# Joining the float32 work of TensorE into longer groups, with a new order of the front

## The chip, the cores and the metric

The kernel runs on one core of a Trainium2 chip. The core has a matrix engine (PE, with its weight loads shown apart as PEld), a vector engine (DVE), a scalar engine (ACT), GpSimd (POOL) and SyncE (SP), whose queue here issues most of the transfers. The metric is device time in microseconds (us) of one execution, as the median over several executions.

## The reference

Three stages follow one another on 8 x 576 = 4608 tokens. First comes a two-step attention with 8 heads of width 64, then a product of two projections, then a two-layer network:

```
p_packed = sm_attn(p, k, v)              # 32 packed queries per head look at all 576 tokens
out      = sm_attn(q, p_packed, p_packed)
x = out as [4608, 512]
x = ((x @ w1) * (x @ w2)) @ w3 @ w_out   # 512 -> 1024 -> 1024 -> 512
h = x @ w_in                             # 512 -> 2048
y = maximum(0.01 * h, h) @ w_out2        # 2048 -> 512
```

`sm_attn` is a softmax attention with scale 1/8. All tensors are float32; the five weight matrices arrive as 64-bit floats, seen by the kernel as pairs of 32-bit words.

## The kernel before, in words

The program has two halves. The first half, up to about 680 us of the trace, does attention and the first network for the 8 batches; the second half does the last network, with a Strassen-like scheme of seven products, and is the same text before and after.

**The front.** Each 64-bit weight tile of 128 x 512 is loaded (`l.3.i` for w3, `l.o.i` for w_out, `l.w.i` for w1 and w2 together) and turned into float32 in three steps: `c` on ACT (line 274), `B` or `b` on DVE (two instructions, lines 280 and 283), `j` on POOL (line 290). From w3 and w_out the kernel makes W13 = w3 @ w_out by 64 float32 products `w.fc.jc` of 128 x 512 (line 379): `w.fc.jc` needs w3 tile `2*fc + jc//4` and w_out tile `jc`. The order of all this, together with attention of batches 0 and 1 and the network of batch 0, is a list written by hand, SCRIPT. `l` takes its buffers in turn from 3 tiles "c64" and from halves of the tiles "M", which are not needed for M yet.

**M.** The packed keys and values of a batch are used in a rewritten form: M = p_packed times (w1, w2), made in four parts f = 0 to 3 by `m_mm` (line 163, by way of `eights`: eight float32 products of 64 rows x 32 columns that fill the array side by side, each seen twice in the trace). `m_hi` (ACT, line 401) and `m_lo` (DVE, line 135) then split M into two reduced float32 parts, and `ab_mm` multiplies them with the attention weights in three passes of 288 columns (line 130): 12 products for one unit A. A unit gives one tile of a and one of b, which are multiplied on DVE (`ab_mul`, line 433) and split again. 16 such units and then 8 units `x2_mm` of 24 products each (line 130, with W13) make the 24 slots of a batch.

**Attention beside it.** While batch b goes through its 24 slots, attention of batch b + 1 is put behind the units of given slots by `attention(b)`: scores with the packed queries (`s1_mm`, line 163, 32 in the trace), maximum, exponential, the transposes of the probabilities (`t_mm`: four of 128 tokens, line 202, and one of the last 64, line 203), their copies, the sums of v (`pv_mm`, line 221: four products of 128 rows x 32 columns for each of four groups of 128 tokens, and four of 64 rows for the last 64 tokens), then a second scores step (`s2_mm`). The heads are treated in two sets g = 0, 1.

**What sets the order.** On TensorE the helper `together` ties the instructions of a float32 group to one another, so that nothing comes between them. Otherwise a scheduler orders each engine's instructions by the order of the code and by modelled times; each engine then runs its list strictly in that order. Tiles come from small pools: in PSUM there are two tiles "at" of two banks (for scores, transposes, sums of v and M) and four "mm" of one bank (for A and x2). In SBUF there are two tiles "M", two "P" (probabilities), two "PT" (transposed), five "v", four "raw" (k and q).

Of the kernel before, what the change touches and what calls it, by code (L numbers as in the profile page):

```python
# [31 lines left out]
Mh.1.0 Ah.4.1 Ml.1.0 A.0.7.0 Al'.4.1 Aa.6.0 Am.6.0 Ah.6.0 A.0.7.1 Aa.7.0 Al'.6.0 Am.7.0 Ah.7.0 S.1 Aa.7.1 Al'.7.0
Am.7.1 Ah.7.1 U.0.0.0 Al'.7.1 D.1.0 k.2.1 k.2.0 D.1.1 E.1.0 A.0.6.1 Us.0.0.0 U.0.0.1 Aa.6.1 Am.6.1 E.1.1 N.1.0 Ah.6.1
U.0.0.2 Us.0.0.1 Al.6.1 X.1.0 x.1.0 N.1.1 U.0.1.0 Us.0.0.2 X.1.1 U.0.1.1 x.1.1 Us.0.1.0 U.0.1.3 Us.0.1.1 U.0.0.3
Us.0.1.3 U.0.1.2 Us.0.0.3 Us.0.1.2
# [9 lines left out]
P = 128  # L45
# [3 lines left out]
TH = 288  # L49
# [6 lines left out]
def tile_kernel(ctx, tc, qT, kT, vL, pT, w12, w3b, wo1, win, wo2, out):  # L56
# [141 lines left out]
    def t_mm(b, g):  # L198
        pt = Ps.pop((b, g))
        t = ps_at()  # L200
        for c in range(4):
            nc.tensor.transpose(t[:, 0, c * P:(c + 1) * P], pt[:, c:512:4], ident)  # L202
        nc.tensor.transpose(t[:64, 1, :P], pt[:, 512:576], ident)
        PTs[b, g] = t

    def t_copy(b, g):
        t = PTs[b, g]
        PT = att.tile([P, 5, P], F32, tag="PT", name="PT", bufs=2)
        nc.scalar.copy(PT[:, 0:4].rearrange("p c s -> p (c s)"), t[:, 0])
        nc.scalar.copy(PT[:64, 4], t[:64, 1, :P])  # L210
        PTs[b, g] = PT

    def pv_mm(b, g):
        PT = PTs.pop((b, g))
        ps = ps_at()[:, 0]
        for c in range(5):
            K = P if c < 4 else 64
            for j in range(4):
                r = slice(j * 32, j * 32 + 32)
                v = vs[b, j // 2, j % 2]  # L220
                ins = nc.tensor.matmul(  # L221
                    ps[r, :64], PT[:K, c, r], v[:K, c, g * 64:g * 64 + 64], start=c == 0, stop=c == 4
                )
                together(ins, c + j == 0)
        pvq[b, g] = ps
# [260 lines left out]
    def attention(b):  # L486
# [4 lines left out]
        d[2] += [lambda: s1_mm(b)]  # L491
        for g in range(2):
            d[2] += [lambda g=g: s1_max(b, g)]
            d[3] += [lambda g=g: s1_exp(b, g)]
            d[4] += [lambda g=g: s1_norm(b, g)]
            d[4 + g] += [lambda g=g: load_kq("q", b, g)]
            d[5 + g] += [lambda g=g: t_mm(b, g), lambda g=g: t_copy(b, g)]
            d[9 + 2 * g] += [lambda g=g: pv_mm(b, g), lambda g=g: pv_scale(b, g)]
        d[12] += [lambda: pp_mm(b), lambda: pp_copy(b)]
# [7 lines left out]
        d[21] += [lambda: m_unit(b, 0)]  # L507
# [5 lines left out]
    def rest_of_m(b):  # L513
        return {4 * f - 4: [lambda f=f: m_unit(b, f)] for f in range(1, 4)}
# [376 lines left out]
```

## Time and profile before

| | us |
|---|---|
| median of three runs | 1295.27 (1294.71 to 1297.86) |
| profiled execution, its own time | 1297.09 |
| span of the profiled execution | 1295.3 |
| PE busy (97% of the span) | 1262.9 |
| DVE busy (67%) | 870.8 |
| ACT busy (47%) | 609.3 |
| POOL busy (8%) | 102.4 |

Busy times are sums over the instructions of one engine. In the rows below a line of a timeline begins with the start time and the length of a merged group of instructions; the lengths overlap a little, since one product begins while the last one drains, so what a group costs is read from its start to the start of the next group. The square bracket at a line's end is idle time before the group and what ended it. PEclk is the granted share of TensorE's full clock. The trace shows the products of line 130 also as f32.

### The profile page before, as it was taken

The page shows a single profiled execution, that of the slowest core. Times are in us where ns is not written, and L with a number is a line of the kernel's source. Part 1 is how long each engine was busy: PE and PEld are TensorE (multiplying, and loading weights), DVE is VectorE, ACT ScalarE, POOL GpSimd, SP SyncE. Part 2 cuts the span into 40 slices and gives each one's busy share as a digit, 9 for nine tenths or more (in the row PEclk, how much of TensorE's full clock was granted, in tenths as well). Part 3 has the DMA queues.
Part 4 walks back from the last instruction along what each step waited for, and adds up shares of the span by engine and source line. Part 5 has one row for each costly group of instructions (what it writes and reads, how often), then busy time and mean ns, then how long its engine had stood idle before and what let it go on. Part 6 is the DMA issues. An engine that isn't in the chain of part 4 may idle for free.

```text
span 1295.3 us, 23350 instructions
## 1 busy us (share of the span) xinstructions
PE 1262.9 (97%) x8984; PEld 1170.3 (90%) x8984; DVE 870.8 (67%) x1449; ACT 609.3 (47%) x1141; POOL 102.4 (8%) x87
## 2 busy tenths in 40 slices
PE   5989999999999999999999999999999998999998
PEld 2458998989898989999999999999999998999998
DVE  5887465676766767648866774676457549586667
ACT  3445344454545454546565555454433343443342
POOL 4543011111110101000000000000000000000000
PEclk9999999999999999999999999999999999999999
DMA  9944244566665745468789776484754583878873
GB/s 351 350 154 160 66 159 140 194 218 220 208 219 164 242 137 187 144 216 273 256 306 318 279 255 219 130 285 147 268 198 144 195 283 105 310 267 294 303 258 122
DMA packets 139375, 283.08 MB, mean 219 GB/s; under 512 B 14848, under 2 KB 66048, under 8 KB 139264
## 3 DMA queue, kind: packets, MB, share of 16 engines
q1 hardware_dynamic: 130048, 272.16, 61.2%
q10 hardware_dynamic: 9216, 9.44, 2.2%
q8 instruction: 70, 1.15, 0.4%
q14 instruction: 41, 0.34, 0.1%
HBM read 202.38 MB, written 79.17 MB: 217 GB/s over the span
## 4 chain that ended last, share of the span: by engine, by line
PE 87%; DMA 8%; DVE 2%; issue 1%; SPq 1%; ACT 1%; POOL 0%; ACTq 0%; DVEq 0%; POOLq 0%
PE mm L130 30%; PE b L746 28%; PE c L746 14%; PE a L746 7%; PE mm L379 4%; PE at L163 4%; DMA xh<-xfd 2%; DMA xfd<-xt 1%; DMA v<-vL 1%; PE at L221 1%; PE at L202 0%; DMA raw<-kT 0%; DMA xfd<-xr 0%; DMA wi<-wid 0%; DMA xfd<-P 0%
## 5 line engine op out<-in xcount | busy, mean ns | idle before, releaser
L130 PEld LDWEIGHTS mm<-AT,M 128*128 128x128 f32 x1536 | 207.9, 189 | 30.2 <-issue 11.7
L130 PE MATMUL mm<-AT,M 128*128 128x288 f32 x1536 | 223.5, 300 | 3.8 <-DVE M L135 2.9
L746 PE MATMUL b<-xh,wi 128*128 128x384 f32 x768 | 219.1, 335 | 0.0
L746 PE MATMUL b<-gh,wo 128*128 128x384 f32 x768 | 214.1, 335 | 3.4 <-DVE o L704 2.7
L130 PEld LDWEIGHTS mm<-ab,W 128*128 128x128 f32 x1536 | 203.5, 188 | 8.3 <-ACT x2s L454 4.2
L130 PE MATMUL mm<-ab,W 128*128 128x288 f32 x1536 | 207.4, 295 | 0.0
L746 PEld LDWEIGHTS b<-gh,wo 128*128 128x128 f32 x768 | 140.3, 188 | 4.7 <-DVE o L704 3.3
L746 PEld LDWEIGHTS b<-xh,wi 128*128 128x128 f32 x768 | 141.0, 188 | 0.3 <-ACT gr L706 0.2
L746 PE MATMUL b<-gl,wo 128*128 128x384 f32 x384 | 128.4, 334 | 0.7 <-DVE gl L135 0.7
L746 PE MATMUL b<-xl,wi 128*128 128x384 f32 x384 | 128.4, 334 | 0.0
L746 PE MATMUL c<-xh,wi 128*128 128x384 f32 x384 | 107.6, 339 | 3.8 <-DMA xh<-xfd 3.8
L539 ACT CAST gh<-gr 128x1152 fp32r<-128x1152 f32 (+1 forms) x72 | 75.5, 1052 | 69.0 <-PE b L746 56.6
L746 PE MATMUL c<-gh,wo 128*128 128x384 f32 x384 | 106.9, 335 | 0.9 <-DVE o L704 0.9
L433 DVE TENSOR_TENSOR ab<-mm,a 128x288 f32<-128x288 f32 x128 | 57.8, 454 | 60.7 <-PE mm L130 40.6
L135 DVE TENSOR_TENSOR gl<-gr,gh 128x1152 fp32r<-128x1152 f32 (+1 forms) x72 | 87.5, 1220 | 11.5 <-ACT gh L539 11.4
L539 ACT CAST gh<-gs 128x1152 fp32r<-128x1152 f32 (+1 forms) x54 | 56.8, 1053 | 57.3 <-PE b L746 31.7
L135 DVE TENSOR_TENSOR ab<-ab,ab 128x288 fp32r<-128x288 f32 x119 | 59.8, 507 | 31.4 <-ACT ab L438 29.6
L694 ACT ACTIVATE gr<-gr 128x1152 f32<-128x1152 f32 (+1 forms) x54 | 57.3, 1062 | 47.0 <-DVE gr L709 46.8
L438 ACT CAST ab<-ab 128x288 fp32r<-128x288 f32 x128 | 55.0, 432 | 50.9 <-DVE ab L433 50.8
L746 PEld LDWEIGHTS c<-xh,wi 128*128 128x128 f32 x384 | 70.9, 190 | 5.1 <-DMA xh<-xfd 4.2
L379 PE MATMUL mm<-ab,w 128*128 128x512 f32 x128 | 61.6, 635 | 14.1 <-POOL ab L290 9.6
L746 PEld LDWEIGHTS b<-gl,wo 128*128 128x128 f32 x384 | 72.1, 188 | 1.0 <-DVE gl L135 1.0
(119 smaller groups left out, 2020.6 us busy)
## 6 DMA issues: line engine op xcount, KB each, us to landing
xh<-xfd SPq DMA_DIRECT2D x126, 384.0 KB, 5.7
xl<-xfd SPq DMA_DIRECT2D x126, 384.0 KB, 5.4
part<-o SPq DMA_DIRECT2D x48, 384.0 KB, 3.0
o<-part SPq DMA_DIRECT2D x48, 384.0 KB, 4.1
c<-wo SPq DMA_DIRECT2D x20, 512.0 KB, 5.2
xfd<-xt SPq DMA_DIRECT2D x49, 192.0 KB, 3.1
xfd<-xr SPq DMA_DIRECT2D x49, 192.0 KB, 2.8
raw<-kT SPq DMA_DIRECT2D x32, 288.0 KB, 5.7
```

The source lines that it names most:

```text
L130: ins = nc.tensor.matmul(dst, lhs(i), rhs(j), start=first and n == 0, stop=last and n == 2)
L135: engine.tensor_tensor(out=out, in0=x, in1=rd(hi), op=ALU.subtract)
L163: ins = nc.tensor.matmul(dst(h)[c * 32:c * 32 + 32], lhs[r, c, :], rhs(c)[r], start=True, stop=True)
L221: ins = nc.tensor.matmul(ps[r, :64], PT[:K, c, r], v[:K, c, g * 64:g * 64 + 64], start=c == 0, stop=c == 4)
L379: nc.tensor.matmul(w13p[fc], words["3", i][:, c:c + P], words["o", jc], start=w13n[fc] == 1, stop=w13n[fc] == 8)
L433: nc.vector.tensor_tensor(out=t, in0=pb[:, :TH], in1=a, op=ALU.mult)
L438: nc.scalar.copy(t[:, 0], ab32[fc, th])
L539: nc.scalar.copy(hi[step], x[step])
L694: nc.scalar.activation(out=out, in_=x, func=AF.Prelu, alpha=0.01)
L746: nc.tensor.matmul(dst, lhs(l), rhs(r), start=first and n == 0, stop=last and n == total - 1, skip_group_check=True)
```

## The change

- M is made in pairs of parts: `m_pair` issues the two float32 groups back to back and then does the two splits; the pool "M" has three tiles. Parts 0 and 1 of the next batch stay at slot 21 (part 1 was at slot 0), parts 2 and 3 go to slot 4 (3 was at slot 8).
- The transposes of both sets g are issued as one group at slot 7 (they were at slots 5 and 6), the sums of v of both sets as one group at slot 10 (they were at 9 and 11). The scores step moves from slot 2 to slot 1, and with it the loads of q and the softmax; the transpose of p_packed moves from 12 to 13.
- The last 64 tokens are padded to 128: "P" and "v" get zeros from POOL (one memset for each set's "P" and one for each of a batch's four "v" tiles, where there were none), the fifth transpose and the last four sums of v run on all 128 rows, and one copy of 640 columns takes the place of two.
- In the front the loads rotate over 3 + 6 buffers in place of 3 + 4, and SCRIPT is in another order. It holds the same steps; in addition part 1 of M for batch 1, and one split of attention (`x'`) goes from DVE to POOL. Of the 16 low splits of batch 0's units nine are on POOL in either order, not the same nine.

```
-l.3.0 l.o.1 l.o.2 l.o.0 l.o.4 l.o.3 l.3.1 v.0.1 c.3.0 B.3.0 p.0 v.0.0 j.3.0 c.o.1 B.o.1 l.3.4 k.0.1 k.0.0 j.o.1 c.o.2
+l.3.1 l.o.5 l.3.5 l.o.4 l.o.6 l.3.7 l.o.3 l.o.7 k.0.0 c.3.1 B.3.1 c.o.5 B.o.5 j.3.1 l.o.2 c.3.5 B.3.5 k.0.1 j.o.5
...
+            nc.gpsimd.memset(t[64:, 4], 0.0)
...
-        pt = att.tile([P, S], F32, tag="P", name="P", bufs=2)
+        pt = att.tile([P, 5 * P], F32, tag="P", name="P", bufs=2)
+        nc.gpsimd.memset(pt[:, S:], 0.0)
...
-            nc.tensor.transpose(t[:, 0, c * P:(c + 1) * P], pt[:, c:512:4], ident)
-        nc.tensor.transpose(t[:64, 1, :P], pt[:, 512:576], ident)
+            together(nc.tensor.transpose(t[:, 0, c * P:(c + 1) * P], pt[:, c:512:4], ident), g + c == 0)
+        together(nc.tensor.transpose(t[:, 1, :P], pt[:, 512:], ident))
...
-        nc.scalar.copy(PT[:, 0:4].rearrange("p c s -> p (c s)"), t[:, 0])
-        nc.scalar.copy(PT[:64, 4], t[:64, 1, :P])
+        nc.scalar.copy(PT.rearrange("p c s -> p (c s)"), t.rearrange("p a s -> p (a s)")[:, :5 * P])
...
-            K = P if c < 4 else 64
...
-                    ps[r, :64], PT[:K, c, r], v[:K, c, g * 64:g * 64 + 64], start=c == 0, stop=c == 4
+                    ps[r, :64], PT[:, c, r], v[:, c, g * 64:g * 64 + 64], start=c == 0, stop=c == 4
...
-                together(ins, c + j == 0)
+                together(ins, g + c + j == 0)
...
-            n = loads[0] % (C64 + 4)
+            n = loads[0] % (C64 + 6)
...
-        m = main.tile([P, 2, 2, 512], F32R, tag="M", name="M", bufs=2)
+        m = main.tile([P, 2, 2, 512], F32R, tag="M", name="M", bufs=3)
...
-    def m_unit(b, f):
+    def m_pair(b, f):
         m_mm(b, f)
-        m_hi(b, f)
-        m_lo(b, f)
+        m_mm(b, f + 1, False)
+        for x in (f, f + 1):
+            m_hi(b, x)
+            m_lo(b, x)
...
-        d[21] += [lambda: m_unit(b, 0)]
+        d[21] += [lambda: m_pair(b, 0)]
...
-        return {4 * f - 4: [lambda f=f: m_unit(b, f)] for f in range(1, 4)}
+        return {4: [lambda: m_pair(b, 2)]}
```

The first place is the queue of SP in the front, from its sixth load on (c and M are load buffers, w3b and wo the 64-bit w3 and w_out, raw takes k, pks the packed queries). Before:

```order
L315 DMA M<-w3b 128x1024
L155 DMA v<-vL 128x512
L156 DMA v<-vL 64x128
L155 DMA v<-vL 128x512
L156 DMA v<-vL 64x128
L143 DMA pks_79<-pT 128x128
L155 DMA v<-vL 128x512
L156 DMA v<-vL 64x128
L155 DMA v<-vL 128x512
L156 DMA v<-vL 64x128
L315 DMA c_126<-w3b 128x1024
L148 DMA raw<-kT 128x576 x4
```

and of the changed kernel, from its sixth load too:

```order
L315 DMA M<-w3b 128x1024
L315 DMA M<-wo 128x1024 x2
L148 DMA raw<-kT 128x576 x2
L315 DMA M<-wo 128x1024
L148 DMA raw<-kT 128x576 x2
L315 DMA c_142<-w3b 128x1024
L315 DMA c_152<-w3b 128x1024
L143 DMA pks_79<-pT 128x128
L315 DMA c_172<-w3b 128x1024
L155 DMA v<-vL 128x512
```

Before, nine loads of v and p stood between the seventh and the eighth weight tile; now v comes behind the twelfth weight tile, and k between the eighth and the tenth.

The second place is PE in a batch of the loop, from the M group behind slot 4 to the sums of v (a row x8 here is x16 in the trace). Before:

```order
L163 MATMUL at<-w,ppT_77 32x512 x8
L130 MATMUL mm<-AT,M 128x288 x12
L202 MATMUL at<-ident,P 128x128 x4
L203 MATMUL at<-ident,P 64x128
L130 MATMUL mm<-AT,M 128x288 x18
L202 MATMUL at<-ident,P 128x128 x4
L203 MATMUL at<-ident,P 64x128
L130 MATMUL mm<-AT,M 128x288 x18
L163 MATMUL at<-w,ppT_77 32x512 x8
L130 MATMUL mm<-AT,M 128x288 x12
L221 MATMUL at<-v,PT 32x64 x20
L130 MATMUL mm<-AT,M 128x288 x24
```

and of the changed kernel:

```order
L164 MATMUL at<-w,ppT_77 32x512 x16
L130 MATMUL mm<-AT,M 128x288 x36
L204 MATMUL at<-ident,P 128x128 x4
L205 MATMUL at<-ident,P 128x128
L204 MATMUL at<-ident,P 128x128 x4
L205 MATMUL at<-ident,P 128x128
L130 MATMUL mm<-AT,M 128x288 x36
L221 MATMUL at<-v,PT 32x64 x40
L130 MATMUL mm<-AT,M 128x288 x24
L233 MATMUL at<-ident,pp 128x128
```

Two M groups stand together, then three A units of 12, both sets of transposes, three units, both sums of v.

The third place is DVE behind that M group (M<-at is the low split of one part, ab_n<-mm the product of a unit, cT the integer step of a weight tile for the second half). Before:

```order
L433 TENSOR_TENSOR ab_2469<-mm,a 128x288
L135 TENSOR_TENSOR ab<-ab_2469,ab 128x288
L135 TENSOR_TENSOR M<-at,M 128x1024
L433 TENSOR_TENSOR ab_2510<-mm,a 128x288
L135 TENSOR_TENSOR ab<-ab_2510,ab 128x288
L280 TENSOR_SCALAR cT<-c_2201 128x512
L433 TENSOR_TENSOR ab_2552<-mm,a 128x288
```

and of the changed kernel:

```order
L433 TENSOR_TENSOR ab_2494<-mm,a 128x288
L135 TENSOR_TENSOR ab<-ab_2465,ab 128x288
L135 TENSOR_TENSOR ab<-ab_2494,ab 128x288
L135 TENSOR_TENSOR M<-at,M 128x1024 x2
L433 TENSOR_TENSOR ab_2543<-mm,a 128x288
L433 TENSOR_TENSOR ab_2572<-mm,a 128x288
L135 TENSOR_TENSOR ab<-ab_2543,ab 128x288
```

Both low splits stand in front of the products of the next two units.

## Rows read from the trace of the kernel before

**Rows 1.** Busy us of each engine in three stretches, clock, DMA share, GB/s.
```profile
core 0: us, PE busy (x) PEld busy (x) DVE busy (x) ACT busy (x) POOL busy (x), PEclk, DMA share, GB/s
16.60:26.00 9.40, 5.92 (x39) 1.90 (x39) 2.77 (x4) 2.02 (x3) 2.54 (x2) 0.82 0.99 379
26.00:80.60 54.60, 53.97 (x238) 24.26 (x238) 48.99 (x79) 23.96 (x45) 29.31 (x23) 1.00 0.77 285
102.00:620.00 518.00, 517.77 (x4709) 471.66 (x4709) 341.74 (x653) 259.46 (x577) 49.87 (x41) 1.00 0.56 184
```

**Rows 2.** Timeline of PE in the front: start, length, group, idle before it.
```profile
15.12 1.13 PE L379 MATMUL mm<-ab,w 128*128 128x512 f32 x2 [0.72 <-POOL ab L290]
16.64 1.13 PE L379 MATMUL mm<-ab,w 128*128 128x512 f32 x2 [0.39 <-POOL w L290]
21.21 3.63 PE L379 MATMUL mm<-ab,w 128*128 128x512 f32 x4 [3.44 <-POOL w L290]
24.77 1.20 PE L163 MATMUL at<-raw,pks 64*32 64x288 f32 x32
...
29.96 6.28 PE L379 MATMUL mm<-ab,w 128*128 128x512 f32 x14 [0.63 <-POOL w L290]
```

**Rows 3.** Waits of DVE from 0 to 81 us: total, times, longest.
```profile
DVE ct L280 <- DMA c<-w3b: 7.7, 2, 4.6
DVE ct L280 <- DMA c<-wo: 3.2, 2, 3.0
DVE st L180 <- PE at L163: 1.9, 1, 1.9
```

**Rows 4.** Line 280 (one each weight tile): us, DVE busy, clock, DMA share, GB/s.
```profile
0.00:38.40 38.40, 11.05 (x16) 0.96 0.96 357
```

**Rows 5.** Timeline of PE behind the first two M groups.
```profile
86.28 4.69 PE L130 MATMUL mm<-AT,M 128*128 128x288 f32 x22 [2.66 <-DVE M L135]
```

**Rows 6.** Timeline of PE with M groups (line 163, x16) between runs of line 130.
```profile
112.50 1.09 PE L163 MATMUL at<-w,ppT 64*32 64x512 f32 x16
113.52 1.85 PE L130 MATMUL mm<-AT,M 128*128 128x288 f32 x12
115.31 1.09 PE L163 MATMUL at<-w,ppT 64*32 64x512 f32 x16
116.33 5.02 PE L130 MATMUL mm<-AT,M 128*128 128x288 f32 x36
121.28 1.20 PE L163 MATMUL at<-raw,ppT 64*32 64x288 f32 x32
122.41 0.40 PE L130 MATMUL mm<-ab,W 128*128 128x288 f32 x1
```

**Rows 7.** The same, the second half of an M group, and the next run.
```profile
169.15 0.64 PE L163 MATMUL at<-w,ppT 64*32 64x512 f32 x8
169.71 0.40 PE L130 MATMUL mm<-AT,M 128*128 128x288 f32 x1
```

**Rows 8.** The same, one sum of v: 128-row part, 64-row part, next run.
```profile
171.49 0.65 PE L221 MATMUL at<-v,PT 128*32 128x64 f32 x32
...
172.07 0.32 PE L221 MATMUL at<-v,PT 64*32 64x64 f32 x8
172.32 0.40 PE L130 MATMUL mm<-AT,M 128*128 128x288 f32 x1
```

**Rows 9.** The same, two sets of transposes and the run between them.
```profile
162.66 0.64 PE L202 MATMUL at<-ident,P 128*128 128x128 f32 x4
...
163.16 2.64 PE L130 MATMUL mm<-AT,M 128*128 128x288 f32 x18
165.63 0.63 PE L202 MATMUL at<-ident,P 128*128 128x128 f32 x4
```

**Rows 10.** Timeline of DVE: a low split of M.
```profile
170.94 1.23 DVE L135 TENSOR_TENSOR M<-at,M 128x1024 fp32r<-128x1024 f32 x1 [0.58 <-ACT M L401]
```

**Rows 11.** The only larger memset of POOL, by line.
```profile
masks.py:197 POOL MEMSET ident<- 128x128 f32 x1 | 0.2, 204 | 0.3 <-POOLq L881 0.3
```

More of the change, by code (lines that the diff above doesn't have):

```diff
@@ L32 @@
[L32 to L35, printed above, removed]
+l.3.1 l.o.5 l.3.5 l.o.4 l.o.6 l.3.7 l.o.3 l.o.7 k.0.0 c.3.1 B.3.1 c.o.5 B.o.5 j.3.1 l.o.2 c.3.5 B.3.5 k.0.1 j.o.5
+c.o.4 B.o.4 w.0.5 j.3.5 c.o.6 l.3.6 B.o.6 w.2.5 j.o.4 c.3.7 l.3.0 B.3.7 w.2.4 j.o.6 c.o.3 p.0 w.0.4 B.o.3 j.3.7 c.o.7
@@ new lines @@
+w.0.6 l.3.4 w.2.6 v.0.0 B.o.7 j.o.3 w.3.4 w.3.5 j.o.7 c.o.2 B.o.2 w.3.6 j.o.2 w.3.7 l.o.0 w.0.7 c.3.6 B.3.6 l.o.1
+w.2.7 c.3.0 B.3.0 s.0 j.3.6 l.3.10 l.3.12 c.3.4 B.3.4 w.3.3 j.3.0 v.0.1 w.3.2 m.0.0 j.3.4 w.0.3 l.3.11 m.0.1 e.0.0
+w.0.2 l.3.2 B.o.0 e.0.1 t.0.0 c.o.0 w.2.2 l.3.13 B.o.1 c.o.1 j.o.0 t.0.1 c.3.10 q.0.0 w.2.3 B.3.10 T.0.0 j.o.1 w.0.0
+c.3.12 q.0.1 B.3.12 j.3.10 w.0.1 T.0.1 l.3.14 l.3.9 y.0.0 n.0.1 wh.0 j.3.12 n.0.0 c.3.11 B.3.11 y.0.1 l.w.0 Y.0.0
+w.2.1 Y.0.1 B.3.2 j.3.11 c.3.2 l.3.3 z.0 w.3.0 Z.0 c.3.13 B.3.13 v.1.1 j.3.2 w.2.0 w.3.1 wl.0 wh.2 j.3.13 wl.2 w.5.7
@@ new lines @@
+wh.3 l.3.15 wl.3 w.5.6 c.3.14 B.3.14 w.6.5 l.w.7 S.0 c.3.9 B.3.9 j.3.14 l.w.5 w.1.2 D.0.0 l.3.8 j.3.9 w.5.2 c.3.3
+w.6.7 k.1.0 w.5.4 p.1 B.3.3 k.1.1 E.0.0 w.1.0 w.6.4 c.3.15 B.3.15 j.3.3 p.2 w.5.5 w.6.6 B.w.7 j.3.15 v.1.0 w.1.5 B.w.5
+w.1.6 c.3.8 w.1.4 N.0.0 w.1.1 w.5.0 w.5.3 B.3.8 X.0.0 w.1.7 x'.0.0 w.1.3 D.0.1 w.5.1 wh.1 j.3.8 w.6.3 c.w.0 c.w.5
+w.6.0 wl.1 wh.5 j.w.5 w.6.2 E.0.1 wl.5 w.6.1 c.w.7 N.0.1 w.7.7 j.w.7 l.w.6 wh.6 l.w.1 l.w.2 w.7.2 w.7.5 wl.6 X.0.1
+w.7.4 B.w.0 w.4.2 c.w.6 w.4.7 B.w.6 j.w.0 l.w.3 c.w.1 w.4.4 B.w.1 j.w.6 w.4.1 c.w.2 w.4.5 B.w.2 j.w.1 l.w.8 w.7.6
@@ L36 @@
+X.1.0 U.0.0.3 Mh.1.0 x.1.0 N.1.1 Ah.4.1 Al'.4.1 U.0.1.0 Us.0.0.3 Ml.1.0 X.1.1 x.1.1 U.0.1.2 Us.0.1.0 U.0.1.3 Us.0.1.2
+U.0.1.1 Us.0.1.3 M.1.1 Us.0.1.1 U.0.0.2 Mh.1.1 Ml.1.1 Us.0.0.2
 """
@@ L185, in s1_exp @@
         st = stats[b, g]
-        pt = att.tile([P, S], F32, tag="P", name="P", bufs=2)
+        pt = att.tile([P, 5 * P], F32, tag="P", name="P", bufs=2)
+        nc.gpsimd.memset(pt[:, S:], 0.0)
         nc.scalar.activation(
-            out=pt.rearrange("p (a s) -> p a s", a=2), in_=s1q[b][g][:, :, :TH], func=AF.Exp, bias=st[:, 1:2],
+            out=pt[:, :S].rearrange("p (a s) -> p a s", a=2), in_=s1q[b][g][:, :, :TH], func=AF.Exp, bias=st[:, 1:2],
             scale=SCALE, accum_out=st[:, 2:3],
@@ L311, in conv_load @@
             if (n - C64) % 2 == 0:
-                spare[:] = [main.tile([P, 2, 2, 512], F32R, tag="M", name="M", bufs=2).bitcast(U32)]
+                spare[:] = [main.tile([P, 2, 2, 512], F32R, tag="M", name="M", bufs=3).bitcast(U32)]
             m = spare[0][:, (n - C64) % 2]
@@ L490, in attention @@
         d[1] += [lambda: load_v(b, 1)]
-        d[2] += [lambda: s1_mm(b)]
+        d[1] += [lambda: s1_mm(b)]
         for g in range(2):
[L493 to L499, printed above, removed]
+            d[1] += [lambda g=g: s1_max(b, g)]
+            d[2] += [lambda g=g: s1_exp(b, g)]
+            d[3] += [lambda g=g: s1_norm(b, g)]
+            d[3 + g] += [lambda g=g: load_kq("q", b, g)]
+            d[7] += [lambda g=g: t_mm(b, g)]
+        for g in range(2):
+            d[7] += [lambda g=g: t_copy(b, g)]
+            d[10] += [lambda g=g: pv_mm(b, g)]
+        for g in range(2):
+            d[10] += [lambda g=g: pv_scale(b, g)]
+        d[13] += [lambda: pp_mm(b), lambda: pp_copy(b)]
         d[16] += [lambda: s2_mm(b)]
```

33 lines of the change are left out of this document (12 added, 21 removed).

## The prediction

> **What bounds the kernel now.** I read the busy times by stretch first, then PE's timeline in the front, then DVE's waits, and last PE's timeline in the batch loop, from start to start of the groups. From 102 to 620 us PE is busy 517.77 of 518.00 us [rows 1]: there the end moves by what leaves PE's list, as long as DVE (341.74 us) and ACT (259.46) still deliver in time. From 26.0 to 80.6 PE has 53.97 of 54.6 us and DVE 48.99, in two-instruction steps with short gaps between them [rows 1]: two engines are full at once. Before that nobody is: from 15 to 30 us PE waits 0.72, 0.39, 3.44 and 0.63 us for converted weight tiles [rows 2], and DVE in its turn waits for the transfers of weight tiles, 7.7 and 3.2 us [rows 3]. The 3.44 us are followed by 3.56 us for four passes (21.21 to 24.77), though fourteen take 6.28 later, 0.45 each [rows 2]: about 1.8 us lost, in a stretch whose mean granted clock was 0.82 of the full 2.4 GHz, so partly at the half level [rows 1]. The second half of the program stands in the same order on each engine, and I cost it at nothing.
>
> **M in pairs.** In the loop all work of PE lies on the path. A run of 36 products of line 130 takes 121.28 - 116.33 = 4.95 us, one of 12 between two M groups 115.31 - 113.52 = 1.79 [rows 6]. So a product costs (4.95 - 1.79) / 24 = 0.132 us, and leaving and re-entering such runs 1.79 - 12 x 0.132 = 0.21 us. An M group costs 113.52 - 112.50 = 1.02 us [rows 6], its second half with the way out 169.71 - 169.15 = 0.56 [rows 7], so its first half 0.46. The scores show what a half costs inside a longer group: four halves of 288 columns take 122.41 - 121.28 = 1.13 us [rows 6]. With halves in proportion to columns, 4h + e = 1.13 and 2 x (512/288) x h + e = 1.02 give h = 0.25 and a way out e = 0.14; a half of M is then 0.44. A second M inside a group costs 2 x 0.44 to 2 x 0.46 in place of 1.02 + 0.21, which saves 0.31 to 0.35; I take 0.33. Of 31 M groups (batch 0 has its first two together already) 18 are left: 13 x 0.33 = 4.3 us.
>
> **Sums of v.** The 128-row part takes 172.07 - 171.49 = 0.58 us, the 64-row part 172.32 - 172.07 = 0.25 [rows 8]. By the scores' h a step of 64 columns is 0.25 x 64/288 = 0.055. Eight steps are 0.44, so the change to 64 rows costs 0.14, as much as the way out; padded, ten steps and the way out are 0.69 in place of 0.83. Padding saves 0.14 for each sum, joining two saves a way out and a re-entry, 0.14 + 0.21 = 0.35. Twelve sums, six pairs, lie in the loop: 12 x 0.14 + 6 x 0.35 = 3.8 us. The four of batches 0 and 1 stand where DVE binds too, and I count them at nothing (0 to 0.9).
>
> **Transposes.** One set takes 163.16 - 162.66 = 0.50 us, the 18 products behind it 2.47, which is 18 x 0.132 + 0.10 [rows 9]: 0.60 in all, five times 0.12. There is no way in or out to be saved, and none at the last transpose, which had 64 columns; joining and padding them is worth 0 (0 to 0.2 for all). The Trainium skill, "TensorEngine Tiling (Array Packing)", Key Properties, says that changing the tiling mode drains TensorE. The trace agrees for the sums of v (0.14) and not for the transposes; by the rule these would give up 16 x 0.14 = 2.2 us more, and the time would be 1281, inside the range of the forecast.
>
> **What this needs elsewhere.** The pair's two low splits are 1.23 us each [rows 10], one behind the other ahead of the next two units' products. PE has 36 products, 4.7 us, until the transposes want the pair's PSUM tiles, and two units, 3.2 us, until it wants an "mm" tile back that waits behind the splits. In the trace DVE reaches such a split 0.58 us early and waits for ACT [rows 10], so the second split ends some 2.5 us behind the pair and the product follows at about 3.0: it fits, by 0.2 us. The third M tile only makes room for the pair. The 48 memsets are new on POOL; the nearest row is 128 x 128 in 0.20 us [rows 11], so at most 10 us of an engine with 102 busy, and they wait for the same buffers as the loads beside them: 0, with a bound of +2 where one holds up the integer joins behind it. The single copy for two saves ACT time off the path.
>
> **The front.** The old order has the eighth weight tile behind nine loads of v and p; the new one has it ahead of them, and its first eight tiles allow 12 of the 64 products, against 5 of the old order's first seven. So the four waits (5.2 us) and the lost 1.8 can go: 7.0 us by PE. By DVE it is at most the two transfer waits less the first landing at 4.6 us, plus 1.9: 8.2 us [rows 3]. But then transfers set the pace: to the nineteenth tile the new queue moves 19 x 0.524 + 1.2 (k) + 1.2 (v) + 0.1 MB = 12.4, which at the 357 GB/s of [rows 4] is 35 us, and DVE is through with it at about 38.4. By then the old order had started 16 [rows 4]. Three tiles at 2 x 0.69 us and the gaps are 4.1 to 4.6 us, and from there DVE is full in either order. I take 4.5. The wait of 2.66 us for the low split of the first M [rows 5] stays: two splits and two tiles' integer steps are still queued there. Bounds of the front: +4 (another wait like the 3.44 us) and -8.2.
>
> **Sum.** 4.3 + 3.8 + 4.5 = 12.6 us. From the profiled execution's own 1297.09 us (span 1295.3 and 1.8 around it) that gives 1284.5. Its time is 1.8 above the median of the three runs, so 1282.7 as a median; I say 1283.
>
> **Rivals.** (a) The front gains nothing: v now comes late, behind weight tiles, and the new loads move the wait from the 8th to a later tile, or DVE, full from 26 us on, gives it all back. For it: the two full engines of [rows 1]; against it: the DVE waits of [rows 3] that have nothing to do with the second half of the front. 1295.3 - 8.1 = 1287.
>
> (b) What PE saves in the loop turns into waits, because DVE and ACT now get their work in bursts; the front gives little. For it: only 0.2 us of slack behind a pair; against it: both engines are busy under 70% of the loop [rows 1]. Half of 8.1 and 0 to 1 of the front are left: 1290 to 1295, around 1293.
>
> (c) Slower. The pair takes both "at" tiles at once and two evacuations queue on DVE in front of the units' products. If DVE is not early at the pair but x late, PE stands still for x - 0.2 at the third unit behind each of the seven pairs at slot 4, and for another x - 2.2 (4.7 - 2.5 is its slack) at the six transposes behind them. At x = 1.5 that is 7 x 1.3 = 9 us, and the loop's gain of 8.1 is gone; at x = 3 it is 7 x 2.8 + 6 x 0.8 = 24 us against 12.6: 1307. It makes the kernel slower by more than 3.9 us from x = 2.4 on (7 x 2.2 + 6 x 0.2 = 16.6). The row of the split speaks against it, since DVE is early there [rows 10]. The Trainium skill, "TensorEngine Tiling (Array Packing)", PSUM Bottleneck, warns of this kind: faster tiled products do not speed up the emptying of PSUM. In this trace PE does not wait for M's PSUM in the loop, so it does not show yet.
>
> (d) The order on PE shows the groups joined, so the change does what it says; that a joined group stops inside for its second "at" tile is part of (b).
>
> **How the numbers follow.** My forecast, 1279 to 1287 with the front between 1 and 8, has 0.57. A front that also loses its waits behind the first M groups (1275 to 1279) has 0.07. (a), 1286 to 1289, has 0.17, (b) 0.11, and (c) 0.08. What this kernel's measurement can tell from no change is about 0.3%, 3.9 us: faster is under 1291.4. The first three cases are faster, 0.81; of (b) nearly all is the same, 0.12 with the edges; slower is 0.07. The range for 8 in 10 is 1276 to 1292; it holds the forecast, (a) and a part of (b).
>
> **What would show it.** Right: M groups of 32 at 1.90 us from start to start; a sum of v pair x80 at about 1.25 us in place of 2 x 0.83; 36-product runs between them still at 4.9; no wait of PE between 15 and 26 us over 1 us; the first M group at about 76 us in place of 80.60. Wrong: PE waits for DVE's M or ab in the loop, over 1 us a batch; DVE waits for weight transfers between 20 and 40 us for over 6 us in total; or a half of M in the pair at over 0.55 us.

## The result, and the profile after

| | before | after |
|---|---|---|
| median (us) | 1295.07 (1294.71 to 1297.86, 4 runs) | 1280.06 (1278.65 to 1282.92, 4 runs) |
| span of the profiled execution | 1295.3 | 1276.9 |
| PE busy | 1262.9 | 1247.5 |
| DVE busy | 870.8 | 868.8 |
| POOL busy | 102.4 | 113.8 |

The ratio is 0.9882, with a 95% interval of 0.986 to 0.9904: the kernel became 15.0 us faster, where 12.3 (1295.27 to 1283) had been forecast. The median lies inside the forecast of 1279 to 1287.

The front first. Busy time by stretch of the kernel after, the second stretch ending at its first M group (columns as in [rows 1]):

```profile
16.60:26.00 9.40, 9.40 (x52) 3.93 (x52) 7.28 (x12) 3.13 (x5) 7.06 (x8) 1.00 1.04 390
26.00:76.16 50.16, 46.81 (x222) 20.83 (x221) 44.46 (x72) 23.53 (x43) 28.86 (x29) 1.00 0.84 298
102.00:620.00 518.00, 516.01 (x4716) 480.60 (x4715) 346.12 (x660) 262.19 (x569) 52.66 (x65) 1.00 0.57 189
```

From 16.6 to 26 us PE is now busy all the time (5.92 of 9.40 us before), at the full clock. PE's timeline of the kernel after, its start and then the place of the first M groups:

```profile
8.60 2.07 PE L379 MATMUL mm<-ab,w 128*128 128x512 f32 x2 [8.60 <-POOL ab L290]
10.88 11.28 PE L379 MATMUL mm<-ab,w 128*128 128x512 f32 x22 [0.20 <-POOL w L290]
22.09 1.20 PE L164 MATMUL at<-raw,pks 64*32 64x288 f32 x32
...
38.77 2.81 PE L379 MATMUL mm<-ab,w 128*128 128x512 f32 x6 [1.79 <-DVE W L135]
...
76.16 1.95 PE L164 MATMUL at<-w,ppT 64*32 64x512 f32 x32 [1.49 <-DVE W L135]
78.47 0.53 PE L130 MATMUL mm<-AT,M 128*128 128x288 f32 x2 [0.35 <-ACT M L401]
80.51 3.18 PE L130 MATMUL mm<-AT,M 128*128 128x288 f32 x22 [1.51 <-DVE M L135]
```

24 passes of W13 run before the scores, with one wait of 0.20 us in place of the four of [rows 2], and the first M group starts at 76.16 (80.60 before). Two new waits come later, of 1.79 and 1.49 us, both for DVE's splits of W13; between 38.4 and 80.6 us PE had waited for nothing before (42.20 of 42.20 us busy). So PE's gain in the front is partly given back. The wait of DVE for the first transfers stays, here in the waits of DVE up to 76.5 us (total, times, longest):

```profile
DVE ct L280 <- DMA c<-w3b: 8.0, 5, 4.3
```

What changed is how many tiles DVE has taken up by 38.4 us: 19 at 373 GB/s, where [rows 4] had 16 at 357. Line 280 alone, from the start to 38.4 us:

```profile
0.00:38.40 38.40, 13.20 (x19) 1.00 0.98 373
```

Now a batch of the loop, in PE's timeline (answers to [rows 6 to 9]):

```profile
271.76 1.95 PE L164 MATMUL at<-w,ppT 64*32 64x512 f32 x32
273.64 5.05 PE L130 MATMUL mm<-AT,M 128*128 128x288 f32 x36
278.53 0.63 PE L204 MATMUL at<-ident,P 128*128 128x128 f32 x4
279.00 0.27 PE L205 MATMUL at<-ident,P 128*128 128x128 f32 x1
279.11 0.65 PE L204 MATMUL at<-ident,P 128*128 128x128 f32 x4
279.59 0.27 PE L205 MATMUL at<-ident,P 128*128 128x128 f32 x1
279.62 5.00 PE L130 MATMUL mm<-AT,M 128*128 128x288 f32 x36
284.55 1.32 PE L221 MATMUL at<-v,PT 128*32 128x64 f32 x80
285.81 3.45 PE L130 MATMUL mm<-AT,M 128*128 128x288 f32 x24
```

From start to start the M pair takes 273.64 - 271.76 = 1.88 us, the ten transposes 1.09, the pair of sums 285.81 - 284.55 = 1.26, and the runs of 36 products between them 4.89 and 4.93, with no wait. DVE behind that pair:

```profile
274.12 2.35 DVE L135 TENSOR_TENSOR M<-at,M 128x1024 fp32r<-128x1024 f32 x2 [0.45 <-ACT M L401]
276.39 0.45 DVE L433 TENSOR_TENSOR ab<-mm,a 128x288 f32<-128x288 f32 x1
```

DVE was 0.45 us early and waited for ACT, as in [rows 10]. The product of the next unit began 2.75 us behind the pair's end and ended 3.20 us behind it.

The 2.0 us that PE is idle between 102 and 620 us are two waits. One of 1.51 us is in the last batch, below. The other is 0.48 us in batch 5, for a unit's product. DVE did that product behind an instruction of the second half's preparation, which itself had waited for its load, in DVE's timeline:

```profile
411.89 0.56 DVE L541 TENSOR_TENSOR PT<-v 128x384 f32<-128x384 f32 x1 [2.05 <-DMA v<-x2d]
```

The last batch looks different. PE's timeline there:

```profile
512.77 1.95 PE L164 MATMUL at<-w,ppT 64*32 64x512 f32 x32
514.65 13.27 PE L130 MATMUL mm<-AT,M 128*128 128x288 f32 x96
529.14 1.85 PE L130 MATMUL mm<-AT,M 128*128 128x288 f32 x12 [1.22 <-DVE ab L433]
531.28 3.53 PE L130 MATMUL mm<-AT,M 128*128 128x288 f32 x24 [0.29 <-DVE ab L433]
```

PE waits 1.51 us for DVE, where the kernel before waited for nothing. The preparation of the second half's weights (tiles wi) starts on DVE here, first after and then before:

```profile
518.57 0.55 DVE L541 TENSOR_TENSOR xr<-wi,wi 128x384 f32<-128x384 f32 x1
542.55 0.55 DVE L535 TENSOR_TENSOR xr<-wi,wi 128x384 f32<-128x384 f32 x1
```

That is 13.8 us behind the first product of the last batch (504.74) after, and 21.8 us (520.78) before.

The two profiled spans, cut at the starts of the same instructions of PE (the last one is the start of its last product, 4.1 us ahead of the end of either span):

| stretch | before | after | difference |
|---|---|---|---|
| start to the first M group | 80.60 | 76.16 | -4.4 |
| first M group to batch 1's first product | 68.79 | 65.32 | -3.5 (and one M group more, about 1.2) |
| batch 1 to batch 7 | 371.39 | 363.26 | -8.1 |
| batch 7 to the second half | 54.65 | 55.23 | +0.6 (and one M group less) |
| second half | 715.78 | 712.79 | -3.0 |

The last line is no effect of the change: its instructions are the same in all kernels here, and its time lay between 710.6 (experiment 5) and 716.6 (experiment 1) in their profiles. The same kernel after, profiled twice more as the control of experiments 9 and 10, gave 711.65 and 710.82.

### The profile page after: what moved, and what is told of

Its sections match the earlier page's. It is cut to its first block, busy times and chain, and to the rows that moved or that the text cites. A ratio compares the mean times of both kernels' runs of the same rounds, so it can differ in the third digit from the quotient of the medians.

```text
span 1276.9 us, 23452 instructions
## 1 busy us (share of the span) xinstructions
PE 1247.5 (98%) x8984; PEld 1167.4 (91%) x8984; DVE 868.8 (68%) x1448; ACT 608.3 (48%) x1125; POOL 113.8 (9%) x136
## 4 chain that ended last, share of the span: by engine, by line
PE 91%; DMA 5%; DVE 3%; issue 1%; SPq 0%; ACT 0%; DVEq 0%
PE mm L130 31%; PE b L752 29%; PE c L752 15%; PE a L752 8%; PE at L164 4%; PE mm L379 3%; DMA xh<-xfd 2%; DMA c<-w3b 1%; DMA raw<-kT 1%; PE at L221 1%; DVE wi L135 1%; PE at L204 1%; DMA xl<-xfd 0%; DMA wi<-wid 0%; DMA v<-x2d 0%
## 5 line engine op out<-in xcount | busy, mean ns | idle before, releaser
L130 PE MATMUL mm<-AT,M 128*128 128x288 f32 x1536 | 215.5, 298 | 3.9 <-DVE ab L433 2.0
L135 DVE TENSOR_TENSOR ab<-ab,ab 128x288 fp32r<-128x288 f32 x119 | 54.5, 459 | 30.4 <-ACT ab L438 29.1
L752 PEld LDWEIGHTS b<-xl,wi 128*128 128x128 f32 x384 | 72.1, 188 | 0.0
```

What stands on the lines that cost most here:

```text
L130: ins = nc.tensor.matmul(dst, lhs(i), rhs(j), start=first and n == 0, stop=last and n == 2)
L135: engine.tensor_tensor(out=out, in0=x, in1=rd(hi), op=ALU.subtract)
L752: nc.tensor.matmul(dst, lhs(l), rhs(r), start=first and n == 0, stop=last and n == total - 1, skip_group_check=True)
```

## The experiments

"Theory" in what follows is the prediction's account: PE's groups cost what the profile says, and early weight tiles win the front. Ratios are against the kernel before, on the same chip, with a 95% interval in brackets. The intervals are about 0.2 to 0.3% wide to either side, 2.3 to 3.4 us: two experiments that lie closer than that are told apart by stretches of the trace, not by their times. The medians of experiments 1, 2, 5, 8 and 10 and of both controls lie 0.1 to 1.2 us outside the ranges expected for them, which is within these intervals.

**1. The old front in the kernel after.** SCRIPT of before, with M.1.1 at its end, and the old rotation of load buffers:

```
...
-            n = loads[0] % (C64 + 6)
+            n = loads[0] % (C64 + 4)
```

> The changed kernel with the old order of the front (and part 1 of M of batch 1 at its end) and the old rotation of 3 + 4 load buffers; the loop stays joined. Theory 'two independent sources' (the front gains by the order of its loads, the loop by fewer ways in and out of float32 groups): the first M group stands at 80 to 81 us again in place of 76.2, PE waits 3 to 5 us in all between 15 and 30 us, and the time is 1280.1 + 4.6 + up to 3.3 = 1285 to 1288 us; the loop from the start of batch 1 to that of batch 7 still gains 8 us on the kernel before. Rival 'what the front gains would be given back': 1280 to 1282. Rival 'all from the front': 1292 to 1295.

Measured: 1289.15 us, ratio 0.9946 [0.9925, 0.9966], so the joined groups alone are worth about 7.0 us (4.4 to 9.7). First M group at 80.82, batch 1 to 7 in 363.71. From 16.6 to 30 us PE is busy 9.55 of 13.4 us:

```profile
16.60:30.00 13.40, 9.55 (x50) 3.73 (x49) 5.90 (x10) 3.61 (x7) 4.20 (x5) 0.87 1.00 375
```

**2. The new front in the kernel before.** The new SCRIPT, rotation and third M buffer; no padding and no joining in the loop:

```
-            n = loads[0] % (C64 + 4)
+            n = loads[0] % (C64 + 6)
...
-        return {4 * f - 4: [lambda f=f: m_unit(b, f)] for f in range(1, 4)}
+        return {4 * f - 4: [lambda f=f: m_unit(b, f)] for f in range(1 + (b == 1), 4)}
```

> The kernel before with the new order of the front, its 3 + 6 load buffers and three M tiles; the loop is not joined and nothing is padded (batch 1 makes its part 1 of M in the front, so its loop leaves it out). Theory 'two independent sources': first M group at 76 to 77 us, time 1295.1 - 4.6 - up to 3.3 = 1287 to 1291 us, the loop per batch as before. Rival 'given back': 1294 to 1296 us although the first M group stands early. Rival 'all from the front': 1280 to 1283.

Measured: 1286.62 us, ratio 0.9925 [0.99, 0.995]: 9.7 us (6.5 to 13). First M group at 75.41, batch 1 to 7 in 372.59. The same stretch:

```profile
16.60:30.00 13.40, 13.33 (x68) 6.22 (x67) 11.26 (x19) 7.58 (x16) 8.92 (x8) 1.00 1.04 389
```

By the medians the two halves add up (7.0 and 9.7 against 15.3 for both by the ratio), within their intervals. In the profiles, up to the second half, they fall short: 5.9 and 5.7 us against 15.5 for both. The loop of experiment 2 took 1.2 us more than before, though it has one M group less (1.2 us): PE waits 1.2 us there for DVE's splits of M, and before 0.2. And the kernel after escaped a stretch at the lower clock that both experiments have (experiment 7). So the front's gain goes with the new front and the loop's with the joined groups, but the front's is not quite independent of the loop behind it. Both experiments change the order and the rotation of load buffers together; no run tells these two apart.

**3. M's pairs set apart by one unit.**

```
...
-        d[21] += [lambda: m_pair(b, 0)]
+        d[21] += [lambda: m_unit(b, 0)]
+        d[22] += [lambda: m_unit(b, 1)]
...
-        return {4: [lambda: m_pair(b, 2)]}
+        return {4: [lambda: m_unit(b, 2)], 5: [lambda: m_unit(b, 3)]}
```

> The changed kernel, but the two parts of M of a pair are issued one unit apart (behind slots 21 and 22, 4 and 5), 13 pairs split, three M tiles kept. Theory 'ways in and out': each split costs 0.31 to 0.35 us, 13 of them 4.0 to 4.6: 1284 to 1285 us, and in the trace a part alone takes 1.02 us from start to the next run of line 130, a pair 1.88. Rival 'bursts' (the pair's two low splits hold up the units, so part of the saving is lost again): splitting costs 0 to 2 us, 1280 to 1282, and the waits of PE for DVE in the loop (2.0 us) vanish.

Measured: 1284.68 us, ratio 0.9908 [0.9882, 0.9934]. Batch 1 to 7 takes 368.49 us, 5.2 more, of which PE's waits are 0.75 (1.23 against 0.48). The other 4.5 over 12 pairs are 0.37 each; 0.33 was forecast. Single batches without a wait say 0.36: 61.05 us in place of 60.34, with two pairs in each. PE's timeline there:

```profile
272.55 1.09 PE L164 MATMUL at<-w,ppT 64*32 64x512 f32 x16
273.57 1.85 PE L130 MATMUL mm<-AT,M 128*128 128x288 f32 x12
275.35 1.09 PE L164 MATMUL at<-w,ppT 64*32 64x512 f32 x16
276.37 3.46 PE L130 MATMUL mm<-AT,M 128*128 128x288 f32 x24
```

Two groups of 1.02 against one of 1.88, and one more re-entry of the products (1.78 for twelve, 12 x 0.132 + 0.20): 0.36.

**4. The sums of v set apart.**

```
...
-            d[10] += [lambda g=g: pv_mm(b, g)]
+            d[10 + g] += [lambda g=g: pv_mm(b, g)]
...
```

> The changed kernel, but the sums of v of the two sets are issued one unit apart (slots 10 and 11) in batches 2 to 7, padded as they are. Theory 'ways in and out': six splits of 0.35 us, 2.1 us: about 1282 us; in the trace one padded sum takes 0.69 to 0.70 us to the next run, a pair 1.25. Rival 'joining sums saves nothing, only the padding does': 1280 us, and the two sums apart take 1.25 us together.

Measured: 1280.09 us, ratio 0.9881 [0.9854, 0.9907], no difference from the kernel after. The step itself, in PE's timeline:

```profile
286.49 0.77 PE L221 MATMUL at<-v,PT 128*32 128x64 f32 x40
287.18 1.87 PE L130 MATMUL mm<-AT,M 128*128 128x288 f32 x12
288.98 0.77 PE L221 MATMUL at<-v,PT 128*32 128x64 f32 x40
289.68 0.53 PE L130 MATMUL mm<-AT,M 128*128 128x288 f32 x2
```

The groups cost 0.69 + 0.70 us and the twelve products between them 1.80, which is 12 x 0.132 + 0.21: with 1.26 for the joined pair that is 0.34 for each split, the forecast 0.35. Six of them, 2.1 us, should show in the loop, but it took 363.83 us, only 0.6 more. Batch by batch the price is there: all six take 60.63 or 60.64 us here, and four of the six in the kernel after 60.30 to 60.35, so 0.3 each. The other two in the kernel after take 60.58 and 61.34, 1.2 more in all; the longer one, batch 5, has PE's wait of 0.48 us behind DVE's load and a gap around it. Here no batch has a wait. So the loop pays 1.8 for the splits and is spared 1.2. PE waits in batch 5 in eight of the twelve profiles with the new loop, whole or in part, for 0.5 to 1.2 us. The price is shown in the rows, not in the time.

**5. The last sums of v on 64 rows again**, in the joined group:

```
...
+            K = P if c < 4 else 64
...
-                    ps[r, :64], PT[:, c, r], v[:, c, g * 64:g * 64 + 64], start=c == 0, stop=c == 4
+                    ps[r, :64], PT[:K, c, r], v[:K, c, g * 64:g * 64 + 64], start=c == 0, stop=c == 4
```

> The changed kernel, but the sums of v of the last 64 tokens run on 64 rows again (memsets, padded transposes and copies stay). Theory 'change of the tiling': each set pays 0.14 us for 128 to 64 rows, and inside a pair again on the way back to 128 rows: a pair takes 1.25 + 0.28 to 0.42 = 1.53 to 1.67 us from start to the next run in place of 1.25, 2 to 3 us in all, about 1282 to 1283 us. Rival 'padding is free both ways, only joining counts': a pair stays at 1.25 us and the time at 1280.

Measured: 1281.17 us, ratio 0.989 [0.9866, 0.9914]. The pair in PE's timeline:

```profile
286.58 1.73 PE L222 MATMUL at<-v,PT 128*32 128x64 f32 x80
288.24 2.00 PE L130 MATMUL mm<-AT,M 128*128 128x288 f32 x13
```

1.66 us against 1.26: 0.40 for a pair, three changes between 128 and 64 rows at 0.13 to 0.14 each. Batch 1 to 7 took 365.66 us, 2.4 more, which is six times 0.40. Unpadded, the joined pair costs just twice a single sum of before (2 x 0.83, [rows 8]): its gain from joining would be only the 0.21 of a re-entry. Padding and joining are worth their 0.62 together.

**6. No padding at all**: as in experiment 5, the memsets away, the fifth transpose with 64 columns, and two copies.

```
...
-        together(nc.tensor.transpose(t[:, 1, :P], pt[:, 512:], ident))
+        together(nc.tensor.transpose(t[:64, 1, :P], pt[:, 512:576], ident))
...
```

> The changed kernel without any padding: sums of v on 64 rows for the last 64 tokens, the fifth transpose with 64 columns, two copies, no memsets; M, sums and transposes stay joined. Theory 'change of the tiling only between row tilings': as the run with 64 rows alone, 1282 to 1283, and two sets of transposes with the run behind them cost the same as padded (ten times 0.12 us). Rival by the drain rule for every change of tiling: the transposes lose 0.14 us for each set on top, 14 to 28 times, 2 to 4 us: 1284 to 1287.

Measured: 1282.18 us, ratio 0.9891 [0.9873, 0.9909]. The transposes in PE's timeline, the last of each set with 64 columns (128*64):

```profile
280.93 0.64 PE L202 MATMUL at<-ident,P 128*128 128x128 f32 x4
281.40 0.27 PE L203 MATMUL at<-ident,P 128*64 128x128 f32 x1
281.51 0.65 PE L202 MATMUL at<-ident,P 128*128 128x128 f32 x4
281.99 0.27 PE L203 MATMUL at<-ident,P 128*64 128x128 f32 x1
282.02 5.00 PE L130 MATMUL mm<-AT,M 128*128 128x288 f32 x36
```

1.09 us, as with the padding: going from 128 to 64 columns in the transposes cost nothing, where going from 128 to 64 rows cost 0.13 to 0.14 in experiment 5. Padding the transposes is worth 0, as forecast. The Trainium skill, "TensorEngine Tiling (Array Packing)", Key Properties, says that a change of the tiling mode drains TensorE. The trace agrees for the rows of the sums and shows no price for the columns of the transposes.

**7. The transposes set apart.**

```
...
-            d[7] += [lambda g=g: t_mm(b, g)]
+            d[6 + g] += [lambda g=g: t_mm(b, g)]
...
```

> The changed kernel with the transposes of the two sets one unit apart (slots 6 and 7), their copies with them. Theory: transposes have no price of a way in or out, so 0 (within 0.3 us in the trace; five transposes are 0.60 us whether alone or in a group of ten): 1280. Rival 'every float32 group pays 0.35': six splits, 2.1 us: 1282.

Measured: 1280.47 us, ratio 0.9879 [0.9858, 0.9901]. Batch 1 to 7 takes 362.78 us with no wait of PE, 363.26 with 0.48 in the kernel after: equal. This run shows something else. Its front is that of the kernel after, instruction for instruction, and so is its wait behind the first M groups, but not what follows:

```profile
80.36 4.71 PE L130 MATMUL mm<-AT,M 128*128 128x288 f32 x22 [1.53 <-DVE M L135]
```

22 products last 4.71 us here and 3.18 in the kernel after. The granted clock from 76 to 92 us, first in this kernel and then in the kernel after (columns as in [rows 1]):

```profile
76.00:92.00 16.00, 14.12 (x133) 11.68 (x134) 14.70 (x24) 9.54 (x20) 8.61 (x10) 0.89 0.71 229
```
```profile
76.00:92.00 16.00, 13.97 (x149) 11.41 (x153) 15.59 (x26) 10.98 (x23) 8.47 (x10) 1.00 0.74 241
```

A mean of 0.89 says that in a part of the 16 us the lower of the two levels (1.2 GHz) was granted. The 1.5 us are clock, and with this front they come or do not come: of the twelve profiles with the new front up to the first M group, five have the 22 products at 4.7 us (experiments 2, 5, 6, 7 and 8) and seven at 3.2 (the kernel after, its two controls, experiments 3, 4, 9 and 10).

**8. The new order up to the first M groups, the old one behind them.** SCRIPT is the new one up to the step P and the old one from there (two weight tiles exchanged to fit).

```
-wl.4 c.w.11 P M.0.1 b.w.8 b.w.11 M.0.0 l.w.10 Mh.0.1 l.w.14 j.w.8 l.w.9 Mh.0.0 Ml.0.1 j.w.11 Ml.0.0 A.0.2.1 c.w.10
+wl.4 c.w.11 P M.0.0 b.w.8 M.0.1 b.w.11 l.w.10 Mh.0.0 l.w.13 j.w.8 l.w.12 Ml.0.0 Mh.0.1 j.w.11 Ml.0.1 A.0.1.1 c.w.10
...
```

> The changed kernel; up to the first M group the new order of the front, from there on the old order of batch 0's units and batch 1's attention (with w tile 13 for 11, and part 1 of M for batch 1 at the end). Theory 'the second part of the front gains by its own order' (it has 1.9 us of PE waits in place of 4.2, and no stretch at half clock behind them): the first M group stays at 75 to 77 us, the stretch from there to the first unit of batch 1 goes from 65.3 to 67.5 to 69.5 us, total 1282.5 to 1284.5. Rival 'it gains because the first part ends earlier and DVE has less left': the stretch stays at 65 to 66 us, 1280.

Measured: 1281.92 us, ratio 0.9891 [0.9871, 0.9911]. First M group at 75.14, from there to batch 1 68.47 us, 3.2 more than after. About 1.5 are the clock (0.89 from 76 to 92 us): against experiment 7, with the same clock there, the stretch is 1.6 us longer (68.47 against 66.85). PE's waits in the stretch are 3.1 us against 1.87. The new ones are one of 0.2 us for ACT's copy of the transposes, and this one:

```profile
PE mm L130 <- DVE st L197: 1.0, 1, 1.0
```

The wait for the M split itself is 1.5 us, as in the kernel after. So 1.2 us come from the order behind the first M groups, 1.5 from the clock, and the cause of 0.5 stays open.

**9. More of the same in the front**, with a control. The first splits of M stand ahead of a weight tile's integer step, M.1.0 beside M.1.1, batch 1's sums of v joined, one more split on POOL:

```
...
-wl.4 c.w.11 P M.0.1 b.w.8 b.w.11 M.0.0 l.w.10 Mh.0.1 l.w.14 j.w.8 l.w.9 Mh.0.0 Ml.0.1 j.w.11 Ml.0.0 A.0.2.1 c.w.10
+wl.4 c.w.11 P M.0.1 b.w.8 M.0.0 l.w.10 Mh.0.1 l.w.14 j.w.8 l.w.9 Mh.0.0 Ml.0.1 Ml.0.0 b.w.11 j.w.11 A.0.2.1 c.w.10
...
```

> The changed kernel once more, beside the next one and on the same chip. Theory: 1279 to 1282 us as before; the end of batch 0 (first product of batch 1) at 141 to 143 us, the spread being a stretch at half the granted clock that comes or does not come after the first M groups (about 1.6 us), as two kernels with the same front showed. No rival: it says how far a difference of one or two us can be read.

> The changed kernel with more of the same in the front: the low splits of the first two M groups stand on DVE ahead of one integer step of a weight tile (they stood behind it), one low split of attention goes from DVE to POOL, M part 0 of batch 1 stands beside part 1, and both sums of v of batch 1 are one group. Theory (PE's order decides, what is joined or waits less is kept): 0.37 for M, 0.35 for the sums of v and up to 1.3 of the 1.5 us wait behind the first M groups: 1.4 to 2.0 us less than the control, 1278 to 1279 us, batch 1's first product 1.4 to 2.0 us earlier at equal clock. Rival (DVE is as full as PE in this stretch, so a split put ahead only makes the next weight tile late): the wait of 1.5 us shrinks but comes back within the next 20 us, and only the 0.7 of the joined groups, or nothing, is left: 1279.5 to 1281.

Measured: 1280.86 us (0.9892 [0.9874, 0.9911]), the control 1278.87 (0.9883 [0.9864, 0.9902]); the times do not tell the two apart. In the traces batch 1 began at 143.15, in the control at 140.65. The three largest new or changed waits of PE from the first M group to batch 1:

```profile
PE mm L130 <- DVE ab L433: 1.3, 1, 1.3
PE mm L130 <- DVE M L135: 0.7, 1, 0.7
PE at L221 <- ACT pp L230: 0.7, 1, 0.7
```

The wait for the split fell from 1.5 to 0.7, and two new ones of 1.3 and 0.7 stand behind it. That is the rival's outcome, and a little worse than it. The rival's reason, a full DVE, does not fit this run: from 76 to 92 us DVE is busy 13.48 of 16 us, in the control 15.44. DVE's timeline shows why:

```profile
77.18 2.36 DVE L135 TENSOR_TENSOR M<-at,M 128x1024 fp32r<-128x1024 f32 x2 [1.28 <-ACT M L401]
```

With the splits put ahead, DVE stood idle for 1.28 us until ACT's half of the split was there. In the control it did a step of a weight tile in that time. Three such steps now came behind the splits and in front of the product that PE then waited 1.3 us for.

**10. The last batch's M apart again**, with a control.

```
...
+        if b == B - 1:
+            return {4: [lambda: m_unit(b, 2)], 8: [lambda: m_unit(b, 3)]}
         return {4: [lambda: m_pair(b, 2)]}
```

> The changed kernel again, beside the next one on the same chip: 1279 to 1281 us; from the first product of the last batch to the second half 55.2 us, of which PE waits 1.5 us for DVE's products of the units, as in all kernels with the pair at slot 4 of the last batch.

> The changed kernel, but in the last batch alone M parts 2 and 3 are made apart at slots 4 and 8, as before the change. Theory: with the last M group at slot 4, DVE's preparation of the second half's weights (40 instructions of 0.55 us on 128 x 384) starts right behind it, among the units of 12 products, which each want two DVE instructions in 1.6 us; PE then waits 1.5 us and loses some 0.6 more around the waits. With the last M at slot 8 the preparation falls among the last units and the steps of 24 products. Parting the pair costs 0.4. From the first product of the last batch to the second half 53.4 to 53.7 us in place of 55.2, no wait of PE over 0.3 us there, and 1.5 to 1.8 us less than the control in all, 1277.5 to 1279. Rival: DVE has the same instructions in this stretch in either order, so PE's wait only moves (to the last units, or to the first products of the second half): 55.2 to 55.7 us, and nothing or 0.4 us more in all.

Measured: 1277.19 us (1274.35 to 1281.23; 0.9865 [0.9843, 0.9887]), the control 1278.62 (1276.78 to 1280.47; 0.9873 [0.9854, 0.9892]). The last batch took 53.43 us against 55.20, 1.8 less, and PE waits for nothing in it:

```profile
513.47 1.09 PE L164 MATMUL at<-w,ppT 64*32 64x512 f32 x16
514.49 6.62 PE L130 MATMUL mm<-AT,M 128*128 128x288 f32 x48
521.04 1.09 PE L164 MATMUL at<-w,ppT 64*32 64x512 f32 x16
```

DVE's preparation of the weights starts at 525.99 us here, 20.6 us behind the first product of the batch (505.44), near the 21.8 of before. The theory holds for the stretch. In the whole time the two kernels are not told apart, since the second half alone moves by more (716.47 in this profile, 710.82 in the control's). The median of this run is the lowest of all kernels run, not a proven lead over the kernel after.

## Why the prediction was right, and where it was not

**The front: 4.5 us forecast, 4.4 measured.** By PE's waits alone it would have been 7.0; 3.3 of new waits for DVE stand against that, at 38.77 and 76.16 us. The tighter bound of the prediction, by the transfers, held: it had 19 weight tiles by 38.4 us, and the row of line 280 shows 19 in all twelve profiles with the new front and 16 in both with the old. The next step of the working is less sure: it took DVE to be full from there on. From 38.4 us to the first M group DVE was busy 37.70 of 42.20 us before and 33.74 of 37.76 after, and the engine without a gap before was PE (42.20 of 42.20; 35.90 of 37.76 after). So three tiles more by 38.4 us are shown, and that they are worth 4.1 to 4.6 us is not. Experiments 1 and 2 tie the gain to the new order with its larger rotation. That 4.4 agrees with 4.5 to a tenth is luck: in those twelve profiles the first M group starts at 74.9 to 77.4 us.

**The loop: 8.1 us forecast, of which 7.8 up to batch 7 (the thirteenth M pair is in the last batch); 8.1 measured there.** Three of the six batches took 61.62 us before, and four 60.30 to 60.35 after: 1.28 a batch, 7.7 in all. The other 0.4 is that the remaining batches were longer by 1.7 in all before and by 1.2 after. M: 0.33 a pair forecast, 0.36 measured (experiment 3). The sums of v: a pair at "about 1.25", measured 1.26; 0.14 for each padding and 0.35 for joining stand in the rows of experiments 4 and 5. Transposes: 0, and 0 (experiments 6 and 7). Reading a group from start to start, and a way out as what its halves leave over, held to within 0.04 us. The margin of 0.2 us behind a pair was not there: ACT's half of the first split ended some 0.5 us behind the pair, which the working had put at nothing, so the two splits on DVE ended some 2.8 us behind it (2.5 forecast) and the product at 3.20 (3.0 forecast), of the 3.2 that PE allows. PE did not wait all the same (36 products in 4.89 us), and rival (c) did not begin; it was nearer than the prediction thought.

**The stretch behind the first M groups: counted at nothing, and wrong.** The prediction had the 2.66 us of [rows 5] stay. It is 3.5 us shorter, though an M group of batch 1 moved into it, which costs 1.2: 4.7 in all. Of these, 2.3 are waits (4.15 before, 1.87 after): the wait for the split fell from 2.66 to 1.51, and the 0.9 us for DVE's statistics of the softmax went, which experiment 8 brings back. About 1.5 are the clock. This stood in the prediction's own row: 22 products in 4.69 us, where its price of 0.132 gives 2.9 [rows 5], or 3.1 with a re-entry. The working used the wait in that row and passed over its length. It was not a sure gain, as experiment 7 shows. About 0.3 are the two padded sums, and 0.6 is not assigned.

**The last batch: counted with the loop, and wrong the other way.** The forecast had one M pair saved there (0.33), and an M group of batch 7 went out of it (1.2); it became 0.6 us longer, a loss of 2.1. When M is done at slot 4 in place of 8, DVE's preparation of the second half's weights starts 8 us earlier in the batch (13.8 us behind its first product in place of 21.8), among the units that need DVE every 1.6 us. This is rival (b), in one batch of eight: the prediction asked what is queued on DVE in the loop, and not what the earlier end of M lets start. Experiment 10 takes it away. A second trace of (b) is the wait of 0.48 us in batch 5, where a load of the second half stands behind DVE's name.

**The sum.** 12.6 + 4.7 - 2.1, and 0.3 for the loop's 8.1 in place of 7.8, is about 15.5, which is the shift of the second half's start (575.43 to 559.97); the medians moved by 15.0. So two terms that were put at nothing or next to it missed by 4.7 and 2.1 in opposite directions, and about 1.5 of the first comes and goes with the clock. That the sum came out within 3 us is in part luck. Rival (a) fell with the front's 4.4, (d) with the rows.

## What to carry to other kernels

Price a change of group from the starts of PE's rows: the ends overlap, and what a half, a way out and a re-entry cost then comes out to a few hundredths of a microsecond. Where a row is longer than its count allows, look at the granted clock before anything else. Where a wait names an engine, look at what that engine itself was waiting for. And when a step is moved forward, look at what its end releases, in the last turn of the loop above all: there the work of the next stage comes in, on an engine that the loop's units also need.

## What the runs showed of the hardware

- Changing between 128 and 64 rows inside a group cost 0.13 to 0.14 us each time (1.66 against 1.26 us for a pair of sums, experiment 5); changing between 128 and 64 columns in transposes cost nothing (1.09 us for ten either way, experiment 6).
- A stretch at the lower clock, behind waits of PE of 1.5, 0.35 and 1.5 us, came in one execution and not in another with the same instructions and the same waits up to there (granted clock from 76 to 92 us 0.89 in experiment 7 and 1.00 in the kernel after). It cost 1.5 us (4.71 against 3.18 for 22 products). With the old front, where the last wait is 2.66 us, it was there in both profiles (4.69 and 4.68).
- The second half, the same instructions in every kernel, took 710.6 to 716.6 us in different executions, which is why gains of 1 to 2 us had to be read from stretches.
